# One pair of d_ff chunks by seven products in tiles 3 to 6 of a fused attention and gated FFN kernel

## The chip, the cores and the metric

The kernel runs on one core of a Trainium2 chip. The metric is device time in microseconds; a forecast speaks of the median of several runs. The engines are named as in the profile: PE is TensorE's matmul stream and PEld its weight loads, DVE is VectorE, ACT is ScalarE, POOL is GpSimd and SP is SyncE, which here only issues DMAs. Each engine takes its instructions in the order in which the program lists them, and an instruction that needs another engine's result waits for a semaphore.

## The reference

```python
scores = scale * np.matmul(q, k.transpose(0, 1, 3, 2))      # q, k, v: 8 batches, 8 heads, 576, 64
mask = block_i >= block_j                                    # blocks of 64 positions
scores = np.where(mask, scores, -1000000000.0)
...                                                          # softmax over the last axis
attn_out = np.matmul(attn, v)
x = np.ascontiguousarray(attn_out.transpose(0, 2, 1, 3)).reshape(B * S, H * D)   # 4608 x 512
gate = np.maximum(x @ w_gate, 0.0)                           # w_gate, w_val: 512 x 1536
val = x @ w_val
return (gate * val @ w_out).astype(np.float32)               # w_out: 1536 x 512
```

## The kernel before

The 4608 tokens are worked as nine FFN tiles of 512. Tiles 0 to 7 hold the first 512 tokens of one batch each, and tile 8 the last 64 tokens of all eight. While the FFN of tile j runs, the attention of batch j+1 is laid between its matmuls, so that PE has work without a break.

**The FFN of a tile.** d_ff is cut into 12 chunks of 128. A chunk's gate and value are four matmuls of 512 columns each (`product`, L937), into one PSUM bank each. ACT writes the relu of the gate to SBUF (`relu`, L947), and DVE multiplies it with the value straight from PSUM into the hidden tile `hT` (`hidden`, L957). Both banks are then free again. From tile 2 on (`SEVEN = 2`) the down-projection is done with Strassen's seven products in place of eight, on blocks of two chunks by 256 columns (`seven_products`, L819); the sums of hidden blocks that it needs are made by DVE during the up-projection (`Sums.make_part`, L778).

**The up-projection by seven products.** Tiles 7 and 8 also do three of their six pairs of chunks in the up-projection by seven products (`by_pairs`, `pair`, L1003; chunks 2 and 3, 4 and 5, 6 and 7: `PAIRS = (2, 4, 6)` lists the first of each). Rows of the left matrix are gate and value of the pair, its columns the two halves of d_model; the right matrix is x, with the halves of d_model as rows and two halves of 256 tokens as columns. Sums of weights are made once (`up_sum`, L736) and kept; sums of x are made per tile (`x_sums`, L929). One product is four matmuls of 256 columns. In those tiles no attention of a next batch runs, and the products take banks that belong to the scores.

**Attention.** A round is one pair of heads of one batch; a batch has four rounds. A round begins with a visit of scores (`visit`, L454): PE writes the scores to two double banks `sc` and to two single banks, the first of its matmuls going to `one` and the second to an `ffnp` bank, and ACT takes the exponentials in four instructions: two for the single banks (L466), then one for each double bank (L459, 1024 elements wide). DVE zeroes masked corners (L1228). Later two groups of products with V follow (`head_av`, L589 and L603), one for each head, and DVE normalises each result out of its bank with a reciprocal and two multiplications (L526, L528, L535). A DMA transposes the round's result into `xT`, the FFN's input for the next tile.

**Banks.** PSUM has eight banks: two double `sc` tiles, one `one` and three `ffnp`. Gates and values, the single banks of a visit, the attention products and the down-projection's accumulators share `one` and `ffnp`.

**Order.** The schedule is written out by hand. `ffn_gen` is a generator that yields after each FFN matmul (or pair of matmuls in the products), and the table `AT` says after how many of these steps each piece of attention, loading or weight preparation is placed. For tiles 3 to 6, whose attention is that of batches 4 to 7, the places repeat with 144 steps a tile before compression, and the offsets come from

```python
STEADY = {"s": 2, "e": 8, "c": 15, "a": 22, "b": 26, "x": 26.1}
AT[f"{n}{r}"] = base + 28 * i + p + (5 if i == 3 and n in "abx" else 0)
```

where `s` is a visit with its first three exponentials, `e` its last exponential, `c` the corners, `a` and `b` the two attention products and `x` the transposing DMA of round i. `place_of` translates these places for tiles whose down-projection has fewer steps.

Of the kernel before, what the change touches and what calls it, by code (L numbers as in the profile page):

```python
# [17 lines left out]
def kernel(  # L18
# [89 lines left out]
    def new_bf():  # L108
        return [sb.tile([128, 2048], BF, name=n, bufs=2) for n in ("q_bf", "k_bf")]
# [603 lines left out]
    def up_sum(n, which):  # L713

        if not ups:
            ups["free"] = [
                t[:, 512 * i : 512 * i + 512].rearrange("p (c f) -> p c f", c=2)  # L720
                for two in (new_bf(), new_bf())
                for t in two
                for i in range(4)
            ]
        i, lo = divmod(PAIRS[n], 4)
        f = slice(128 * lo, 128 * lo + 256)
        g, u = wg[i], wv[i]
        a, b, op = {
            1: (g[:, 0:2, f], u[:, 2:4, f], AX.add),
            2: (u[:, 0:2, f], u[:, 2:4, f], AX.add),  # L730
            5: (g[:, 0:2, f], g[:, 2:4, f], AX.add),
            6: (u[:, 0:2, f], g[:, 0:2, f], AX.subtract),
            7: (g[:, 2:4, f], u[:, 2:4, f], AX.subtract),
        }[which]
        t = ups[n, which] = ups["free"].pop(0)
        nc.vector.tensor_tensor(out=t, in0=a, in1=b, op=op)  # L736

    class Sums:
# [58 lines left out]
    def seven_products(j, quads, sums):  # L797

        def times(to, which, p, c, first):
            two = wo[c // 2][:, 2 * (c % 2) : 2 * (c % 2) + 2, :]
            t = sevens[c // 2][:, 768 * (c % 2) : 768 * (c % 2) + 768]
            right = {  # L810
                5: two[:, 1, 256:512],
                2: two[:, 0, 0:256],
                1: t[:, 0:256],
                3: two[:, 0, 256:512],
                4: two[:, 1, 0:256],
                6: t[:, 256:512],
                7: t[:, 512:768],
            }[which]
            nc.tensor.matmul(  # L819
                to,  # L820
                sums.of(c)[which][:, 128 * p : 128 * p + 128],
                right,
                start=first,
                stop=(c == 5),
                skip_group_check=True,
            )

        def half(to, p):
            return to[:, 256 * p : 256 * p + 256]

        early, last = ((0, 1, 2, 3), (4, 5)) if j < B - 1 else ((0, 1, 2, 4), (3, 5))

        def whole(to, which, new=True, cs=range(6)):
            for p in range(2):
                for c in cs:
                    times(half(to, p), which, p, c, new and (p, c) == (0, 0))
                    if c % 2:
                        yield

        def store_later(hi, n0, ob, p0=0, p1=2):  # L840
            if store:
                store.pop()()
            if j < B:
                store.append(lambda: put_block(j, hi, n0, ob, p0, p1))
            else:
                put_block(j, hi, n0, ob, p0, p1)

        y = psum_ffn.tile([128, 512], FP, name="ffnp")
        z = psum_one.tile([128, 512], FP, name="one")
        for to, which in ((y, 5), (z, 2)):  # L850
            yield from whole(to, which, cs=early)
        for to, which in ((y, 5), (z, 2)):
            yield from whole(to, which, new=False, cs=last)
        for q in range(3) if j >= B - 1 else ():
            sums.make_part(q, 1, 0, 2)
        g = sb.tile([128, 512], FP, name="ob", bufs=5)
        nc.scalar.copy(g, y)
        nc.vector.tensor_tensor(out=g, in0=z, in1=g, op=AX.add)
        for q in range(3) if j >= B - 1 else ():
            sums.make_part(q, 2, 0, 2)  # L860
        m1 = psum_ffn.tile([128, 512], FP, name="ffnp")
        yield from whole(m1, 1)
        nc.vector.tensor_tensor(out=g, in0=m1, in1=g, op=AX.subtract)
        if j == B - 1:
            x_sums(B, (1, 3))
        yield from whole(y, 3, new=False)
        c12 = sb.tile([128, 512], FP, name="ob", bufs=5)
        nc.scalar.copy(c12, y)  # L868
        store_later(0, 256, c12)
        c22 = sb.tile([128, 512], FP, name="ob", bufs=5)  # L870
        nc.gpsimd.tensor_tensor(out=c22, in0=g, in1=c12, op=AX.add)  # L871
        yield from whole(z, 4, new=False)
        c21 = sb.tile([128, 512], FP, name="ob", bufs=5)
        nc.scalar.copy(c21, z)
        store_later(1, 0, c21)
        nc.gpsimd.tensor_tensor(out=g, in0=g, in1=c21, op=AX.add)
        m6 = psum_ffn.tile([128, 512], FP, name="ffnp")
        yield from whole(m6, 6)
        nc.vector.tensor_tensor(out=c22, in0=m6, in1=c22, op=AX.add)
        store_later(1, 256, c22)  # L880
        if j < B:
            m7 = psum_ffn.tile([128, 512], FP, name="ffnp")
            yield from whole(m7, 7)
            nc.vector.tensor_tensor(out=g, in0=g, in1=m7, op=AX.subtract)
            store_later(0, 0, g)
        else:
            for p in range(2):
                m7 = psum_ffn.tile([128, 512], FP, name="ffnp")[:, 0:256]
                for c in range(6):
                    times(m7, 7, p, c, c == 0)  # L890
                    if c % 2:
                        yield
                nc.vector.tensor_tensor(
                    out=half(g, p), in0=half(g, p), in1=m7, op=AX.subtract
                )
                store_later(0, 0, half(g, p), p, p + 1)
# [34 lines left out]
    def ffn_gen():  # L931
        for j in range(B + 1):
# [30 lines left out]
            def by_pairs():  # L963
# [8 lines left out]
                def gate(f):  # L972
                    to = psum_ffn.tile([128, 512], FP, name="ffnp")
                    for c in range(4):
                        product(to, 0, c, f)
                        yield
                    gates[f] = relu(to)

                def value(f):
                    to = psum_ffn.tile([128, 512], FP, name="ffnp")  # L980
                    for c in range(4):
                        product(to, 1, c, f)
                        yield
                    nc.vector.tensor_tensor(
                        out=quads[f // 4][:, f % 4], in0=gates[f], in1=to, op=AX.mult
                    )

                def times(to, n, which, new):
# [30 lines left out]
                def pair(n, first, second, third=()):  # L1019
# [37 lines left out]
                        op1=AX.mult,  # L1057
                    )

                while len(sums.two) < 3:  # L1060
                    sums.two.append(sb.tile([128, 2048], BF, name="stage", bufs=10))
                yield from gate(0)
                store.pop()()
                if j < B:
# [20 lines left out]
                yield from value(11)  # L1085
                sums.make_part(2, 0, 1, 2)

            if j >= B - 1:
                yield from by_pairs()
                yield from seven_products(j, quads, sums)  # L1090
                continue
# [141 lines left out]
    with tc.manual_schedule(engines={E.PE, E.DVE, E.Activation, E.Pool, E.SP}):  # L1233
# [371 lines left out]
            "cv00/23": "pool",  # L1605
            "cv01": "pool",
        }
        STEADY = {"s": 2, "e": 8, "c": 15, "a": 22, "b": 26, "x": 26.1}
        acts = {
            "Lq0": lambda: e0.load_qk(0, 2, nc.scalar),  # L1610
            **{f"Lq{h}": lambda h=h: e0.load_qk(h, 2) for h in (2, 4, 6)},
# [89 lines left out]
        for b in range(4, B):  # L1701
            base = 144 * (b - 1)
            for i in range(4):
                r = 4 * b + i
                here = ("sc", "sc") if i == 3 else ("one", "ffn")
                acts.update(round_at(r, ("dve", *here, None)))
                for n, p in STEADY.items():
                    AT[f"{n}{r}"] = base + 28 * i + p + (5 if i == 3 and n in "abx" else 0)
            acts[f"L{b}"] = lambda b=b: last_keys(b)
            AT[f"L{b}"] = base + 11  # L1710
            if b + 1 < B:
                acts[f"l{b + 1}"] = lambda b=b: load_qkv(b + 1, (0, 1), products[-1])
                acts[f"lv{b + 1}"] = lambda b=b: load_qkv(b + 1, (2,))
                acts[f"d{b + 1}"] = lambda b=b: dma_transposes(b + 1)
                for n, p in (("l", 9), ("lv", 46), ("d", 66)):
                    AT[f"{n}{b + 1}"] = base + p
# [4 lines left out]
        acts["X"] = lambda: x_sums(B, (4,))  # L1721
        AT["X"] = 1003
        for i in range(15):
            n, which = i // 5, (5, 2, 1, 6, 7)[i % 5]
            acts[f"U{i}"] = lambda n=n, which=which: up_sum(n, which)
            AT[f"U{i}"] = (
                820 + 5 * i if i < 8 else 878 + 28 * (i - 8) if i < 10 else 964 + 8 * (i - 10)
            )
        for c in range(6):
            AT[f"W{c}"] = (225, 229, 233, 242, 266, 270)[c]  # L1730
# [4 lines left out]
        def place_of(p):  # L1735

            j, o = divmod(p, 144)
            if j < SEVEN:
                return p
            return 144 * SEVEN + 138 * (j - SEVEN) + min(o, 96) + max(0, o - 96) * 42 / 48  # L1740

        for n in sorted(acts, key=lambda n: AT[n]):
            at = int(place_of(AT[n]))
# [33 lines left out]
```

## Time and profile before

| | |
|---|---|
| median of 3 runs | 354.49 us (354.23 to 355.2) |
| the profiled execution | 353.72 us, of which the span of instructions is 351.9 |
| PE busy | 340.1 us, 97% of the span |
| PEld busy | 209.3 us, 59% |
| DVE busy | 224.2 us, 64% |
| ACT busy | 185.9 us, 53% |
| POOL busy | 154.4 us, 44% |
| granted TensorE clock | 0.999 of full speed |
| tiles 3, 4, 5 | 37.39 us each |

Busy times are sums over the span, in which a matmul's record is longer than the time until the next one starts; the time that a matmul costs is read from start to start. Engines overlap, so that the shares don't add up to one. The chain that ended last lies on PE for 89% of the span. In the lines of a timeline the first number is the start in us from the start of the span, the second the time until the end of the last instruction of the row, and a bracket at the end tells how long the engine was idle before and which instruction ended that.

### The profile page before, as it was taken

How to read it: one execution, taken by the hardware profiler on the slowest of the kernel's cores; microseconds unless marked ns; L12 is line 12 of the kernel's file. 1: busy time of each engine (PE TensorE's matmuls, PEld its weight loads, DVE VectorE, ACT ScalarE, POOL GpSimd, SP SyncE). 2: the span in 40 equal slices, each digit the busy share in tenths (PEclk: the TensorE clock that was granted, in tenths of full speed). 3: DMA queues.
4: the chain of work that ended last, by engine and by line, in shares of the span. 5: the costliest groups of instructions: out<-in, count | busy, mean ns of one | idle time of the engine just before them, and what ended most of it. 6: DMA issues, size and time to landing. Idle time of an engine off the chain costs nothing.

```text
span 351.9 us, 8257 instructions
## 1 busy us (share of the span) xinstructions
PE 340.1 (97%) x3202; PEld 209.3 (59%) x3245; DVE 224.2 (64%) x558; ACT 185.9 (53%) x298; POOL 154.4 (44%) x195
## 2 busy tenths in 40 slices
PE   7899999999999999999999999999999999999994
PEld 2544455545454568555855576557755687687674
DVE  4654455658546784467547772668566867885892
ACT  4942756587335861666355546555366515423521
POOL 4847556588956902590149203950300022213213
PEclk9999999999999999999999999999999999999999
DMA  8999999999999996899459944999310031003005
GB/s 241 295 353 374 345 232 270 199 142 172 186 208 103 144 178 130 113 143 165 65 135 140 145 92 125 129 141 141 114 47 15 18 84 60 2 0 122 1 2 119
DMA packets 155399, 50.02 MB, mean 142 GB/s; under 512 B 134464, under 2 KB 151744, under 8 KB 155360
## 3 DMA queue, kind: packets, MB, share of 16 engines
q0 software_dynamic: 70528, 8.98, 46.8%
q1 hardware_dynamic: 76432, 31.47, 44.5%
q10 hardware_dynamic: 8400, 9.05, 8.2%
q8 instruction: 25, 0.41, 0.5%
q14 instruction: 14, 0.11, 0.1%
HBM read 37.75 MB, written 9.44 MB: 134 GB/s over the span
## 4 chain that ended last, share of the span: by engine, by line
PE 89%; ACT 5%; DVE 2%; issue 1%; POOL 1%; POOLq 0%; DVEq 0%
PE ffnp L937 45%; PE ffnp L819 12%; PE ffnp L1168 5%; PE one L819 5%; PE sc L1003 3%; PE sc L454 3%; ACT attnT L418 3%; PE one L454 2%; PE one L589 2%; PE one L1003 2%; PE ffnp L589 2%; PE one L937 1%; PE ffnp L551 1%; PE sc L589 1%; ACT attnT L459 1%
## 5 line engine op out<-in xcount | busy, mean ns | idle before, releaser
L937 PE MATMUL ffnp<-xT,wg 128*128 128x512 bf16 x340 | 93.8, 379 | 0.8
L947 ACT ACTIVATE gate_sb<-ffnp 128x512 bf16<-128x512 f32 x95 | 57.3, 606 | 70.1 <-PE ffnp L937 65.7
L937 PE MATMUL ffnp<-xT,wv 128*128 128x512 bf16 x315 | 90.1, 379 | 1.6 <-issue 0.6
L957 DVE TENSOR_TENSOR hT<-gate_sb,ffnp 128x512 bf16<-128x512 bf16 x78 | 53.3, 684 | 51.6 <-PE ffnp L937 27.0
L459 ACT ACTIVATE attnT<-sc 128x1024 bf16<-128x1024 f32 x56 | 57.5, 1042 | 0.0
L937 PEld LDWEIGHTS <-wv 128*128 128x128 bf16 x384 | 35.0, 98 | 36.6 <-issue 3.7
L937 PEld LDWEIGHTS <-wg 128*128 128x128 bf16 x384 | 35.3, 98 | 35.6 <-issue 2.2
L871 POOL TENSOR_TENSOR ob<-ob 128x512 f32<-128x512 f32 x7 | 9.6, 1371 | 103.0 <-ACT ob L868 54.2
L819 PEld LDWEIGHTS <-stage 128*128 128x128 bf16 x420 | 40.3, 98 | 6.0
L778 DVE TENSOR_TENSOR stage<-hT 128x512 bf16<-128x512 bf16 (+2 forms) x82 | 37.8, 493 | 0.9
L589 PEld LDWEIGHTS <-attnT 128*128 128x128 bf16 x640 | 26.7, 98 | 12.6 <-issue 1.3
L819 PE MATMUL ffnp<-stage 128*128 128x256 bf16 x252 | 31.4, 273 | 0.0
L466 ACT ACTIVATE attnT<-one 128x512 bf16<-128x512 f32 (+1 forms) x28 | 15.0, 536 | 26.4 <-PE ffnp L454 26.4
L342 POOL DMA_DIRECT2D q_bf<-in_q_dram x20 | 18.2, 921 | 22.4 <-DVE hT L957 17.1
L342 POOL DMA_DIRECT2D v_bf<-in_v_dram x30 | 24.1, 849 | 2.0 <-DMA k_bf<-in_k_dram 0.8
L1168 PE MATMUL ffnp<-wo,hT 128*128 128x512 bf16 x90 | 22.4, 379 | 0.2
L454 PEld LDWEIGHTS <-kTm 64*128 64x128 bf16 x384 | 13.1, 94 | 14.3 <-issue 8.3
L1034 POOL TENSOR_TENSOR ob<-ob 128x512 f32<-128x512 f32 x6 | 7.7, 1275 | 23.2 <-ACT ob L1033 20.2
L454 PE MATMUL sc<-qTm,kTm 64*128 64x512 bf16 (+1 forms) x168 | 17.8, 305 | 0.0
L342 POOL DMA_DIRECT2D k_bf<-in_k_dram x20 | 17.7, 922 | 0.0
L819 PEld LDWEIGHTS <-hT 128*128 128x128 bf16 x168 | 16.4, 98 | 1.9
L868 ACT COPY ob<-ffnp 128x512 f32<-128x512 f32 x7 | 4.1, 585 | 22.1 <-PE ffnp L819 22.1
(192 smaller groups left out, 550.3 us busy)
## 6 DMA issues: line engine op xcount, KB each, us to landing
out_dram<-ob ACTq DMA_DIRECT2D x32, 256.0 KB, 2.4
stage<-in_moe_w_val_dram SPq DMA_DIRECT2D x6, 512.0 KB, 8.3
stage<-in_moe_w_gate_dram SPq DMA_DIRECT2D x6, 512.0 KB, 8.7
stage<-in_moe_w_out_dram SPq DMA_DIRECT2D x6, 512.0 KB, 10.6
q_bf<-in_q_dram POOLq DMA_DIRECT2D x20, 128.0 KB, 4.4
k_bf<-in_k_dram POOLq DMA_DIRECT2D x20, 128.0 KB, 5.9
v_bf<-in_v_dram POOLq DMA_DIRECT2D x20, 128.0 KB, 6.4
stage<-in_v_dram SPq DMA_DIRECT2D x19, 128.0 KB, 5.4
```

What stands on the lines that cost most here:

```text
L342: ins = nc.gpsimd.dma_start(dst, part_of)
L454: nc.tensor.matmul(o, kTm[b % 2][head_of(hh), c, hp, :], qT, start=True, stop=True)
L459: return lambda: nc.scalar.activation(at[:, :, lo : lo + 512], sc, AF.Exp, scale=scale)
L466: nc.scalar.activation(at[:, hh, 1024 : 1024 + w], third[hh][:, 0:w], AF.Exp, scale=scale)
L589: nc.tensor.matmul(av[:, p, :], at[:, col : col + 128], v_bf[b % 2][:, c, h, :], start=(p == 0), stop=(c == p), skip_group_check=True,)
L778: nc.vector.tensor_tensor(out=out.rearrange("p (c n) -> p c n", c=m), in0=a, in1=b, op=op)
L819: nc.tensor.matmul(to, sums.of(c)[which][:, 128 * p : 128 * p + 128], right, start=first, stop=(c == 5), skip_group_check=True,)
L937: nc.tensor.matmul(to, (wg, wv)[t][f // 4][:, c, 128 * (f % 4) : 128 * (f % 4) + 128], x[:, c], start=(c == 0), stop=(c == 3),)
L947: nc.scalar.activation(gate_sb, gate, AF.Relu)
L957: nc.vector.tensor_tensor(out=h, in0=gate_sb, in1=val, op=AX.mult)
L1003: nc.tensor.matmul(to[:, 256 * k : 256 * k + 256], left[:, c, 128 * k : 128 * k + 128], right[:, c], start=new and (k, c) == (0, 0), stop= ...
L1168: nc.tensor.matmul(op, hT[f][:, 128 * s : 128 * (s + 1)], wo[f // 4][:, f % 4, n0:n1], start=(f == 0), stop=(f == 11),)
```

## The change

Tiles 3 to 6 now go through `by_pairs` too, but take one pair only, that of chunks 4 and 5 (`PAIRS[1]`), by the seven products. A new function `middle` does it, with two `ffnp` banks (`y`, `z`) and `one` (`m1`), between the second and the third visit of scores. Between its products stand the value of chunk 8, the gate of chunk 9, and the attention products of round 1. The chunks are now worked in the order 0, 1, 2, 3, 8, the pair 4 and 5, 9, 10, 11, 6, 7. The five sums of x are made after the values of chunks 0, 1 and 2. A tile has two steps fewer (94 for its up-projection, not 96), the places of the rounds are listed one by one, and the attention products of round 1 use the banks `sc` and `one`, not `one` and `ffnp`. The weight sums of this pair are made during tile 2 and lie in two buffers of the pool `stage`, which has ten; before, they were made around tiles 5 and 6 and lay in buffers that batch loads had left. The down-projection of tiles 3 to 6 takes the pairs of chunks in the order that tiles 7 and 8 had, with the last chunks last.

```diff
-        early, last = ((0, 1, 2, 3), (4, 5)) if j < B - 1 else ((0, 1, 2, 4), (3, 5))
+        early, last = ((0, 1, 2, 3), (4, 5)) if j == SEVEN else ((0, 1, 2, 4), (3, 5))
...
+                def middle(n, halves):
+                    q, k0 = divmod(PAIRS[n], 4)
+                    h = quads[q][:, k0 : k0 + 2]
+                    y, z, m1 = bank("ffn"), bank("ffn"), bank("one")
+                    low, a, b = ob(), ob(), ob()
+                    yield from times(y, n, 5, True)
+                    nc.scalar.copy(a, y)
+                    yield from times(z, n, 2, True)
+                    nc.vector.tensor_tensor(out=a, in0=z, in1=a, op=AX.add)
+                    yield from halves[0]
+                    yield from times(m1, n, 1, True)
+                    nc.vector.tensor_tensor(out=a, in0=m1, in1=a, op=AX.subtract)
+                    yield from times(y, n, 3, False)
+                    high = relu(y)
+                    yield from halves[1]
+                    yield from times(z, n, 4, False)
+                    nc.scalar.copy(low, z)
+                    yield from times(y, n, 6, False)
+                    nc.vector.tensor_tensor(out=b, in0=y, in1=a, op=AX.add)
+                    yield from times(z, n, 7, False)
+                    nc.vector.tensor_tensor(out=a, in0=z, in1=a, op=AX.add)
...
+                if j < B - 1:
+                    yield from both(0)
+                    x_sums(j, (1, 3))
+                    yield from gate(1)
+                    store.pop()()
+                    yield from value(1)
+                    x_sums(j, (4, 6))
+                    yield from both(2)
+                    x_sums(j, (7,))
+                    yield from both(3)
+                    yield from gate(8)
+                    sums.make_part(0, 0, 0, 2)
+                    yield from middle(1, (value(8), gate(9)))
+                    yield from value(9)
+                    yield from gate(10)
...
-            if j >= B - 1:
+            if j > SEVEN:
                 yield from by_pairs()
...
-        STEADY = {"s": 2, "e": 8, "c": 15, "a": 22, "b": 26, "x": 26.1}
+        STEADY = (
+            (2, 8, 15, 22, 26, 26.1),
+            (30, 38.5, 44, 52, 56, 56.1),
+            (61, 67, 73, 79, 82.5, 82.6),
+            (86, 92, 99, 113, 117, 117.1),
+        )
...
-                here = ("sc", "sc") if i == 3 else ("one", "ffn")
+                here = (("one", "ffn"), ("sc", "one"), ("one", "ffn"), ("sc", "sc"))[i]
...
-            n, which = i // 5, (5, 2, 1, 6, 7)[i % 5]
+            n, which = (1, 0, 2)[i // 5], (5, 2, 1, 6, 7)[i % 5]
...
-                820 + 5 * i if i < 8 else 878 + 28 * (i - 8) if i < 10 else 964 + 8 * (i - 10)
+                390 + 8 * i if i < 5 else 820 + 8 * (i - 5) if i < 10 else 964 + 8 * (i - 10)
```

Two more products of halves, `high` times `b` and the relu of `a` times `low`, end `middle` and write the pair's half of `hT`.

## The prediction

> **What bounds the kernel now.** I read the page's busy line and its chain first, then one row of engine busy time per tile, then the timelines of tile 4 on three engines, because tiles 3 to 6 are the changed ones and look alike.
>
> The page, part 1 and the chain by engine:
>
> ```profile
> PE 340.1 (97%) x3202; PEld 209.3 (59%) x3245; DVE 224.2 (64%) x558; ACT 185.9 (53%) x298; POOL 154.4 (44%) x195
> ...
> PE 89%; ACT 5%; DVE 2%; issue 1%; POOL 1%; POOLq 0%; DVEq 0%
> ```
>
> TensorE (PE) carries the chain. The table by stretch, one tile (its up-projection, down-projection and the attention laid between) to a row; columns: start:end, length, then busy us of each engine:
>
> ```profile
> 141.44:178.83 37.39, 37.02 (x364) 23.22 (x370) 22.71 (x60) 20.23 (x33) 16.31 (x19) 1.00 1.42 129
> 178.83:216.22 37.39, 37.02 (x364) 23.21 (x370) 22.71 (x60) 20.23 (x33) 16.29 (x19) 1.00 1.31 126
> ```
>
> A tile takes 37.39 us, PE is idle for 0.37 of it, VectorE (DVE) works 22.71 and ScalarE (ACT) 20.23. So any PE time saved shows in the total, if PE is not made to wait; and any wait shows in full.
>
> **What the change saves.** PE rows of the timeline (start, length, and a count of matmuls):
>
> ```profile
> 187.23 1.03 PE L937 MATMUL ffnp<-xT,wg 128*128 128x512 bf16 x4
> 188.10 1.03 PE L937 MATMUL ffnp<-xT,wv 128*128 128x512 bf16 x4
> ...
> 212.24 2.78 PE L819 MATMUL ffnp<-stage 128*128 128x256 bf16 x24
> 214.86 0.59 PE L937 MATMUL ffnp<-xT,wg 128*128 128x512 bf16 x2
> ```
>
> Four 512-column matmuls take 188.10 - 187.23 = 0.87 us (0.216 each), and 24 of 256 columns 214.86 - 212.24 = 2.62 (0.109 each). A pair of chunks was 16 of the first kind, 3.46 us; it becomes seven products of four matmuls, 28 of the second, 3.06. Saved: 0.40 us a tile, 1.6 us over four tiles. That is the whole gain.
>
> **What it adds beside PE, per tile.** DVE loses two products `hT` (chunks 4 and 5) and gains five sums of x, two adds from PSUM into `a`, `b = y+a`, `a = z+a`, and two products of halves: nine instructions more, net. ACT loses one relu (four chunk relus become three, counting `high`) and gains two copies. Five weight sums move from tiles 5 and 6 to tile 2's down-projection, where DVE stands idle for 3.03 us before L879; five at 0.42 (the L778 row of 512 elements) are 2.1 us: I cost them at nothing, and at most 2.1 us if that idle time weren't there. The two extra `stage` buffers leave five for the sums, which need four, and a tile's first sum is written long after PE has read the last tile's: nothing. Attention products of round 3 come about 0.65 us later in the down-projection; their transposes (3.5 us to landing, by the DMA part) still have about 2 us before the next tile's third matmul needs them: nothing. The order of partial products over chunks (3 and 5 last) only matches the order in which chunks finish.
>
> **The wait that it adds.** There are three `ffnp` banks. In the middle, `y` and `z` hold two until the end, so one bank serves gate 8, value 8, gate 9 and value 9 in turn. Gate 9 can't start before DVE has done `hT` of chunk 8. In DVE's order that product stands behind `a = z+a`, which needs ACT's copy of `y`, and ACT's copy stands behind the second exponential of the visit. PE waits at the end of that line, so I lay it out on the clock of tile 4 (ACT rows, up to that exponential they do not change, as the second visit keeps its place):
>
> ```profile
> 186.44 0.60 ACT L466 ACTIVATE attnT<-one 128x512 bf16<-128x512 f32 x1 [0.22 <-PE ffnp L454]
> 186.94 0.59 ACT L466 ACTIVATE attnT<-ffnp 128x512 bf16<-128x512 f32 x1
> 187.41 1.03 ACT L459 ACTIVATE attnT<-sc 128x1024 bf16<-128x1024 f32 x1
> 188.31 0.62 ACT L947 ACTIVATE gate_sb<-ffnp 128x512 bf16<-128x512 f32 x1
> 188.79 1.06 ACT L459 ACTIVATE attnT<-sc 128x1024 bf16<-128x1024 f32 x1
> ...
> 212.44 0.58 ACT L874 COPY ob<-one 128x512 f32<-128x512 f32 x1 [0.68 <-PE one L819]
> ```
>
> A 1024-wide exponential holds ACT 0.90 us (187.41 to 188.31). So ACT takes the copy up at 188.79 + 0.90 = 189.69 and ends it at 190.28. DVE rows:
>
> ```profile
> 190.00 0.30 DVE L1228 MEMSET attnT<- 64x128 uint32 x2
> 190.34 0.43 DVE L778 TENSOR_TENSOR stage<-hT 128x512 bf16<-128x512 bf16 x1
> ...
> 191.77 0.20 DVE L526 RECIPROCAL recip<-one 128x5 f32<-128x5 f32 x1
> 192.00 0.42 DVE L528 TENSOR_TENSOR xnat<-one,recip 128x256 bf16<-128x256 f32 x1
> 192.34 0.20 DVE L535 TENSOR_TENSOR xtail<-one,recip 64x64 bf16<-64x64 f32 x1
> 192.47 0.67 DVE L778 TENSOR_TENSOR stage<-hT 128x1024 bf16<-128x1024 bf16 x1
> ...
> 207.78 0.69 DVE L858 TENSOR_TENSOR ob<-one,ob 128x512 f32<-128x512 f32 x1 [0.66 <-ACT ob L857]
> 208.38 0.18 DVE L526 RECIPROCAL recip<-sc 128x5 f32<-128x5 f32 x1
> ```
>
> Reading starts against starts: a 512-wide add from PSUM holds DVE 0.60 (207.78 to 208.38) and is complete after 0.69; two memsets 0.34; one normalisation 0.70 (191.77 to 192.47). Hence `a = z+a` from 190.31, the two corner memsets from 190.91, `hT` 8 from 191.25 to 191.94. I take 0.05 us from a DVE or ACT end to PE (a transpose's weight load starts 0.06 after its `xnat` ends at 57.71). Gate 9 starts at 191.99.
>
> PE without waits: gate 8 ends at 188.10, then products 5 and 2 (0.44 each), value 8 (0.87), products 1 and 3: gate 9 would start at 190.72. Product 3 already waits 0.06 for the copy. **Stall: 1.27 us**, more than three times the saving. Nothing hides it: everything after it on PE is queued behind.
>
> **What is late next.** From gate 9 at 191.99: attention products (0.45), products 4 and 6, attention products, ended at 194.63; product 7 and three matmuls of value 9 bring PE to visit 3 at 195.72. DVE gets the attention result 0.20 later (record ends lag the next issue by 0.16), normalises until 195.53, and then makes `b = y+a` until 196.22. That frees the `ffnp` bank of the visit's second matmul at 196.27, wanted at 195.78: **stall 0.49**.
>
> DVE then has a full queue: `a = z+a` (from 196.25), two products of halves, `hT` 9 at 0.60 each, to 198.65; a half sum, 199.04; `hT` 10 when its relu is there, 199.29; sum 0.62, memsets 0.34, three sums 0.87 (the row at 203.92 is three in 0.95), `hT` 11, three sums again; so it takes up the normalisation of round 2 at 203.19, done 203.97. PE wants that bank for visit 4 at 203.42: **stall 0.60**. Afterwards PE's needs (the bank of chunk 6's product, the first sums for the down-projection) come later than DVE delivers, by 0.2 to 0.5 us. Ahead of the middle, the five sums of x make `hT` 2 late by 0.07 for value 3.
>
> **Sum per tile:** 0.07 + 1.27 + 0.49 + 0.60 - 0.40 = +2.03 us; times four, +8.1. On the profiled execution's 353.72 that gives 361.8; the median of the runs, 354.49, lies 0.77 above that execution, and the forecast for the median is 354.49 + 8.1 = **362.6**. Bounds for the wait latencies that no row of this stretch shows: 0 to 0.2 us at each of four waits, so -0.8 to +2.4 us in all. Sums of x: 0.34 (three in 1.09 us) to 0.56 (two in 1.12, with POOL busy), and up to 0.2 each more can only reach PE through value 3: up to 0.5 a tile, 2 us. I take the low ends, as DVE idles 1.2 us (0.28, 0.41, 0.54) between its first product and its first normalisation of the tile.
>
> **Rivals.**
> 1. *PE stays the only bound and all is covered:* 354.49 - 1.6 = 352.9. For it: DVE is busy only 61% and ACT 54% of a tile. Against: the line above is an order, not a load. It decides where `hT` 8 ends by 190.7, which would need the copy 1.2 us earlier, before the second exponential. Chance 0.05; a halfway case within 0.3% (about 1.1 us, what a measurement of this kernel can tell from no change) 0.02.
> 2. *Only the bank wait counts:* DVE catches up, by its idle 0.25 us and shorter half-width operations, and the stalls at visits 3 and 4 are hidden: 0.07 + 1.27 - 0.40 = 0.94 a tile, 358.3. For it: those two rest on a long chain of 0.60s. Against: a single stall recovered there puts the same DVE work under the next visit. Chance 0.21.
> 3. *DVE becomes the bound into the down-projection:* another 1 us a tile, above 366. For it: margins of 0.2 to 0.5 us. Against: DVE waits 3.03 us for POOL in the down-projection. Chance 0.09.
> 4. *The clock falls when PE waits.* Half speed from gate 9 to visit 3 (3.7 us of PE work) would add 3.7 a tile: 354.49 + 8.1 + 14.8 = 377. The stretch 9:13 us has PE busy 3.04 of 4.00 at a granted clock of 1.00, so pauses of this kind did not do it. The Trainium skill, "TensorE: Matmul & The Clock Gate", section "A second HAM failure mode: psum-queue depth-cycling", says that frequent short PE idling while PSUM banks are cycled can make the clock swing to half; by that rule the time would be rival 4's, and the trace disagrees so far. Chance 0.03.
>
> **Numbers.** Forecast 0.60; slower in all 0.60 + 0.21 + 0.09 + 0.03 = 0.93. The range runs from rival 2 less 1 us to the forecast with 0.2 us at each wait and some more: 357.3 to 365.6; left out are rivals 1, 3 and 4 and the halfway case, 0.19.
>
> **What would show it.** In the profile after: tiles 3 to 6 some 39.4 us long with PE idle 2 to 3 us in each; gate 9 waiting on the `hT` product of chunk 8 for 1.2 to 1.3 us, four times; waits of PE at visits 3 and 4 on DVE; DVE near 27.5 us a tile (22.7 + 5 x 0.42 + 4 x 0.69); granted clock 1.00. I am wrong if gate 9 follows product 3 at once, or if ACT's copy of `y` ends before the second exponential does.

## The result and the profile after

The changed kernel takes 364.06 us (median of 4 runs, 362.99 to 364.21) where the kernel before, run beside it, takes 354.39 (354.23 to 355.2). The ratio is 1.026, with a 95% interval of 1.024 to 1.029. The profiled execution took 364.21 us, with a span of 362.3.

The page of the changed kernel, busy time by engine and then the chain by engine:

```profile
PE 342.7 (95%) x3254; PEld 214.3 (59%) x3293; DVE 242.4 (67%) x606; ACT 188.5 (52%) x302; POOL 154.7 (43%) x195
...
PE 71%; DVE 14%; ACT 8%; issue 2%; DMA 2%; POOL 1%; DVEq 0%; POOLq 0%
```

The span is 10.4 us longer, but PE is busy only 2.6 us longer (342.7 against 340.1). In the chain, PE falls from 89% to 71%, and DVE and ACT rise from 2% and 5% to 14% and 8%. So PE waits for those two, and neither is near full. The table by stretch says the same of one tile (start:end, length, then busy us of PE, PEld, DVE, ACT and POOL, the granted clock, the DMA share and GB/s):

```profile
184.41:224.10 39.69, 37.49 (x378) 24.26 (x380) 26.74 (x72) 20.81 (x34) 16.32 (x19) 1.00 1.12 119
```

The tile takes 39.69 us in place of 37.39, which is 2.30 more. PE is idle for 2.20 us of it, where it was 0.37. DVE works 26.74 us and ACT 20.81, both far under 39.69. From the list of PE's waits, the three that lie in tiles 3 to 6 (what waited, for whom: us in total, times, longest):

```profile
PE ffnp L941 <- DVE hT L989: 4.9, 4, 1.2
PE one L454 <- DVE xtail L535: 2.2, 4, 0.5
...
PE ffnp L454 <- DVE ob L1087: 0.7, 4, 0.2
```

Each came four times, once a tile: gate 9 on the `hT` product of chunk 8, visit 4 on the normalisation, visit 3 on `b = y+a` (L1087). PE's rows in tile 4 give their place and their size. Visit 2, products 1 and 3 with gate 9, visit 3, and value 6 (the L941 row at 206.70) with visit 4:

```profile
189.64 0.28 PE L454 MATMUL one<-qTm,kTm 64*128 64x256 bf16 x1
189.97 0.27 PE L454 MATMUL ffnp<-qTm,kTm 64*128 64x256 bf16 x1
...
190.71 0.60 PE L941 MATMUL ffnp<-xT,wv 128*128 128x512 bf16 x2
...
193.77 0.60 PE L1009 MATMUL one<-perm,stage 128*128 128x256 bf16 x4
194.30 0.60 PE L1009 MATMUL ffnp<-perm,wg 128*128 128x256 bf16 x4
196.13 1.02 PE L941 MATMUL ffnp<-xT,wg 128*128 128x512 bf16 x4 [1.24 <-DVE hT L989]
...
199.96 0.28 PE L454 MATMUL one<-qTm,kTm 64*128 64x256 bf16 x1
200.40 0.27 PE L454 MATMUL ffnp<-qTm,kTm 64*128 64x256 bf16 x1 [0.17 <-DVE ob L1087]
...
201.15 0.39 PE L941 MATMUL ffnp<-xT,wv 128*128 128x512 bf16 x1
...
206.70 1.02 PE L941 MATMUL ffnp<-xT,wv 128*128 128x512 bf16 x4
208.26 0.28 PE L454 MATMUL one<-qTm,kTm 64*128 64x256 bf16 x1 [0.54 <-DVE xtail L535]
```

A bracket counts from the modelled end of the record before it, which lies later than the time at which the next matmul could have started (the four of value 6 end 1.02 us after they start by the record, where four cost 0.87). So I read the waits from start to start, against the same places where nothing waits. Product 3 starts 0.53 after product 1, where a product costs 0.43 to 0.44: 0.10 lost. Gate 9 starts 1.83 after product 3: 1.39 lost, not 1.24. Visit 2 lasts from 189.64 to 190.71, which is 1.07, and visit 3 from 199.96 to 201.15, 1.19. In the trace of before these two visits of tile 4 took 0.84 each, so 0.23 and 0.35 are lost:

```profile
185.95 0.28 PE L454 MATMUL one<-qTm,kTm 64*128 64x256 bf16 x1
186.03 0.28 PE L454 MATMUL ffnp<-qTm,kTm 64*128 64x256 bf16 x1
...
186.79 0.60 PE L937 MATMUL ffnp<-xT,wv 128*128 128x512 bf16 x2
...
193.85 0.28 PE L454 MATMUL one<-qTm,kTm 64*128 64x256 bf16 x1
...
194.69 0.61 PE L937 MATMUL ffnp<-xT,wg 128*128 128x512 bf16 x2
```

Visit 4 starts 1.56 after value 6, where the kernel without that wait shows 0.96 (below): 0.60 lost. Together 0.10 + 1.39 + 0.23 + 0.35 + 0.60 = 2.67 lost, less 0.40 saved: 2.27 of the 2.30.

ACT's and DVE's rows at gate 9 show the line itself, ACT first:

```profile
192.72 1.05 ACT L459 ACTIVATE attnT<-sc 128x1024 bf16<-128x1024 f32 x1
193.62 0.63 ACT L1075 COPY ob<-ffnp 128x512 f32<-128x512 f32 x1
...
194.28 0.69 DVE L1077 TENSOR_TENSOR ob<-ffnp,ob 128x512 f32<-128x512 f32 x1 [1.44 <-ACT ob L1075]
195.06 0.30 DVE L1302 MEMSET attnT<- 64x128 uint32 x2
195.39 0.69 DVE L989 TENSOR_TENSOR hT<-gate_sb,ffnp 128x512 bf16<-128x512 bf16 x1
```

The second exponential holds ACT until 193.62. The copy ends at 194.25, and DVE, idle for 1.44 us by then, starts `a = z+a` at 194.28. The memsets follow, and then the `hT` product, which ends at 196.08. Gate 9 starts at 196.13. DVE waited in the middle of the line that PE waits at the end of: an order, not a load.

From the start of tile 3 to the first product of tile 7 the two traces differ by 9.04 us (156.37 against 147.33), and behind that by nothing (61.21 us to the end, against 61.25). The other 1.40 us of the profiled executions' difference lie ahead of tile 3. There this execution was granted a clock of 0.96 in its first 40 us (1.00 before), and at 96 us the chain goes over a transposing DMA. In nine profiles tile 3 starts at 143.31 to 144.72 us, at 143.32 before and at 143.31 in a kernel (the extra copy below, kernel 6) with all of the change. So that part goes with the execution, and nothing shows it to be the change's.

### The profile page after: what moved, and what is told of

It reads as the page before. It is cut to its first block, busy times and chain, and to the rows that moved or that the text cites. A ratio compares the mean times of both kernels' runs of the same rounds, so it can differ in the third digit from the quotient of the medians.

```text
span 362.3 us, 8396 instructions
## 1 busy us (share of the span) xinstructions
PE 342.7 (95%) x3254; PEld 214.3 (59%) x3293; DVE 242.4 (67%) x606; ACT 188.5 (52%) x302; POOL 154.7 (43%) x195
## 4 chain that ended last, share of the span: by engine, by line
PE 71%; DVE 14%; ACT 8%; issue 2%; DMA 2%; POOL 1%; DVEq 0%; POOLq 0%
PE ffnp L941 30%; PE ffnp L823 11%; PE one L823 5%; DVE stage L782 3%; PE sc L1009 3%; PE ffnp L1242 3%; ACT attnT L459 3%; DVE hT L989 3%; PE sc L454 2%; ACT attnT L418 2%; DMA xT<-xnat 2%; PE one L454 2%; PE one L1009 2%; PE one L589 2%; PE one L941 1%
## 5 line engine op out<-in xcount | busy, mean ns | idle before, releaser
L951 ACT ACTIVATE gate_sb<-ffnp 128x512 bf16<-128x512 f32 x91 | 54.6, 604 | 69.3 <-PE ffnp L941 62.2
L941 PE MATMUL ffnp<-xT,wg 128*128 128x512 bf16 x308 | 84.6, 379 | 6.4 <-DVE hT L989 4.9
L941 PE MATMUL ffnp<-xT,wv 128*128 128x512 bf16 x287 | 80.8, 379 | 0.9
L941 PEld LDWEIGHTS <-wg 128*128 128x128 bf16 x352 | 32.3, 98 | 37.7 <-issue 7.3
L941 PEld LDWEIGHTS <-wv 128*128 128x128 bf16 x352 | 32.7, 98 | 33.0 <-issue 4.1
L989 DVE TENSOR_TENSOR hT<-gate_sb,ffnp 128x512 bf16<-128x512 bf16 x52 | 35.5, 683 | 22.7 <-ACT gate_sb L951 13.6
L961 DVE TENSOR_TENSOR hT<-gate_sb,ffnp 128x512 bf16<-128x512 bf16 x30 | 20.5, 684 | 16.9 <-PE ffnp L941 13.9
```

The costliest lines, as they stand in the source:

```text
L941: nc.tensor.matmul(to, (wg, wv)[t][f // 4][:, c, 128 * (f % 4) : 128 * (f % 4) + 128], x[:, c], start=(c == 0), stop=(c == 3),)
L951: nc.scalar.activation(gate_sb, gate, AF.Relu)
L961: nc.vector.tensor_tensor(out=h, in0=gate_sb, in1=val, op=AX.mult)
L989: nc.vector.tensor_tensor(out=quads[f // 4][:, f % 4], in0=gates[f], in1=to, op=AX.mult)
```

## The experiments

Two theories were set against each other. By the *order theory* the loss is the sum of single waits, each the end of one line of instructions or one bank's turn, and each can be removed by moving an instruction. By the *load theory* DVE and ACT have too much to do in the tile, and a wait removed in one place comes back in another. Each kernel's tile period is read from the start of the same matmul in tiles 4 and 5, and its time is the median of its runs; a ratio is to the kernel before. The first four ran on one chip beside the kernel before (354.27), the last three on another (354.0).

**1. Product first.** `a = z+a` is issued behind the instructions of value 8, so that `hT` 8 no longer stands behind the copy.

```diff
-                    nc.vector.tensor_tensor(out=a, in0=z, in1=a, op=AX.add)
                     yield from halves[0]
+                    nc.vector.tensor_tensor(out=a, in0=z, in1=a, op=AX.add)
```

> The add a = z+a is put behind value 8, so that DVE multiplies chunk 8's hidden tile before it waits for ACT's copy of y. Order theory (gate 9's wait is a line of instructions: second exponential, copy, add, memsets, product): the product can end 0.05 us after the memsets, gate 9 starts some 1.25 us earlier in each of tiles 3 to 6 (its wait falls from 1.24 to 0.1 us), all that follows moves with it: about 359.0 us, 5.0 less than the changed kernel. Load theory (DVE has too much work in these tiles, the wait only shows where it is paid): the waits at visits 3 and 4 grow by what gate 9 gains; 361.5 us or more.

Measured: 359.67 us, ratio 1.0131 (1.0093 to 1.0168). The tile falls from 39.69 to 38.48, by 1.21. PE's rows, product 3 and gate 9 in tile 4:

```profile
191.77 0.60 PE L1009 MATMUL ffnp<-perm,wg 128*128 128x256 bf16 x4
192.40 1.02 PE L941 MATMUL ffnp<-xT,wg 128*128 128x512 bf16 x4
```

Gate 9 now follows after 0.63 us, 0.19 over a product's 0.44. So 1.39 - 0.19 = 1.20 of the wait is gone, and the tile is shorter by just that. The waits at visits 3 and 4 stay at 0.17 and 0.54 by their brackets: what was removed did not come back. This one line is half of the loss.

**2. Sums later.** The three sums of the hidden blocks of chunks 4 and 5 are made behind value 6, not behind value 11, so that the normalisation of round 2 stands ahead of them on DVE.

```diff
-                    sums.make(1, range(3), 0, 1)
...
+                    sums.make(1, range(3), 0, 1)
```

> Only the three half sums of chunks 4 and 5 are moved, from behind value 11 to behind value 6, so that the normalisation of round 2 no longer stands behind them. Order theory: the 0.54 us wait at visit 4 goes, DVE makes these sums while PE is at gate 7: 2.2 us less, about 361.9 us. Load theory: the same work is then late for the first products of the down-projection or the bank of chunk 6: at most 0.5 us less, 363.6 us.

Measured: 361.34 us, ratio 1.019 (1.0153 to 1.0226), and a tile of 39.07, 0.62 less. PE's rows, value 6 and visit 4 in tile 4:

```profile
205.59 1.02 PE L941 MATMUL ffnp<-xT,wv 128*128 128x512 bf16 x4
206.55 0.28 PE L454 MATMUL one<-qTm,kTm 64*128 64x256 bf16 x1
```

They are 0.96 apart, against 1.56: the wait is gone in full, and the sums, made later, delay nobody: the tile is shorter by as much as the wait was long.

**3. Round 0 later.** This one tests a wait that the prediction did not have. Visit 2's second matmul writes the `ffnp` bank that gate 3 held, and it follows the first by 0.33 us, not 0.08 as before. The second attention product of round 0 is placed two steps later, behind gate 3, which gives ACT the time for gate 3's relu.

```diff
-            (2, 8, 15, 22, 26, 26.1),
+            (2, 8, 15, 22, 28, 28.1),
```

> Only the second attention product of round 0 is placed two steps later, behind gate 3, so that gate 3's relu ends before visit 2 wants that bank. The second matmul of visit 2 comes 0.33 us after the first in the changed kernel, 0.08 before the change. Order theory: visit 2 and with it ACT's line to gate 9 start 0.2 to 0.25 us earlier per tile: 0.8 to 1.0 us less, about 363.1 us. If that gap has another cause: no change, 364.1 us.

Measured: 362.05 us, ratio 1.0204 (1.0173 to 1.0234), and a tile of 39.40, 0.29 less. PE's rows, visit 2 and value 8 behind it:

```profile
188.42 0.28 PE L454 MATMUL one<-qTm,kTm 64*128 64x256 bf16 x1
188.42 0.28 PE L454 MATMUL ffnp<-qTm,kTm 64*128 64x256 bf16 x1
...
189.19 0.60 PE L941 MATMUL ffnp<-xT,wv 128*128 128x512 bf16 x2
```

The visit takes 0.77 us, 0.30 less than 1.07, and even 0.07 less than in the kernel before. Four tiles of 0.29 are 1.2 us; the medians differ by 2.0, and the surplus has no place in these tiles.

**4. All orders.** The three edits together, and in round 1 the corners two steps later and the second attention product one step later and in a bank `sc`. DVE then makes `b = y+a`, which frees visit 3's bank, ahead of that product's normalisation and not behind it.

```diff
-            (30, 38.5, 44, 52, 56, 56.1),
+            (30, 38.5, 46, 52, 57, 57.1),
...
-                here = (("one", "ffn"), ("sc", "one"), ("one", "ffn"), ("sc", "sc"))[i]
+                here = (("one", "ffn"), ("sc", "sc"), ("one", "ffn"), ("sc", "sc"))[i]
```

> All of the above at once, and in round 1 the corners two steps later, the second attention product one step later (so that DVE makes b = y+a before it normalises) and in a bank of the scores. The same work as the changed kernel, other orders. Order theory: all four waits shrink to 0.2 us or less a tile and the saving of 0.40 us shows: 353.5 to 355.0 us, at or a little under the kernel before. Load theory: DVE cannot do the added 5 us a tile in the time, 358 us or more.

Measured: 354.34 us, ratio 0.9992 (0.9973 to 1.0011), and a tile of 37.45. With the same work on DVE and ACT (26.64 and 20.80 us a tile) 2.24 of the 2.30 us are gone. The load theory falls. DVE's rows show the new order, `b = y+a` and then the reciprocal of round 1's second normalisation; visit 3 comes at 195.38 and no longer waits:

```profile
193.56 0.69 DVE L1087 TENSOR_TENSOR ob<-ffnp,ob 128x512 f32<-128x512 f32 x1
194.62 0.20 DVE L526 RECIPROCAL recip<-sc 128x5 f32<-128x5 f32 x1 [0.37 <-PE sc L603]
```

PE still waits once a tile, with product 7:

```profile
193.75 0.38 PE L1009 MATMUL ffnp<-perm,stage 128*128 128x256 bf16 x2 [0.28 <-ACT ob L1085]
```

It waits for ACT's copy of `z` (`low`), which can only begin when product 4 has ended, and only product 6 lies between products 4 and 7. Product 6 starts at 192.87, so product 7 is 0.44 late, which is more than the whole saving.

**5. Copy first.** Round 1's second exponential goes behind the copy of `y`, and its first attention product between products 4 and 6.

```diff
-            (30, 38.5, 46, 52, 57, 57.1),
+            (30, 41, 46, 54, 57, 57.1),
```

> The kernel with all orders changed, and round 1's second exponential and first attention product put some steps later (30, 41, 46, 54 in place of 30, 38.5, 46, 52), so that ACT copies the two product sums of the up-projection ahead of that exponential. By the order theory the waits that were left in the all-orders kernel go: product 7's 0.44 us and product 3's 0.1 us a tile, so a tile falls from 37.45 to about 36.9 to 37.1 us and the time from 354.3 to about 352.4 us, 0.5% under the kernel before. By the load theory the tile is as full as its engines allow and the time stays at 354 us or above.

Measured: 352.37 us (7 runs, 352.17 to 353.86), ratio 0.9962 (0.9949 to 0.9975). It is faster than both kernels. Its table by stretch, tile 4; then ACT's copy and second exponential; then PE's product 3 and gate 9:

```profile
180.72:217.72 37.00, 36.69 (x377) 23.94 (x380) 26.56 (x72) 20.69 (x34) 16.29 (x19) 1.00 1.54 127
```

```profile
188.74 0.62 ACT L1075 COPY ob<-ffnp 128x512 f32<-128x512 f32 x1
189.20 1.08 ACT L459 ACTIVATE attnT<-sc 128x1024 bf16<-128x1024 f32 x1
```

```profile
190.22 0.60 PE L1009 MATMUL ffnp<-perm,wg 128*128 128x256 bf16 x4
190.80 1.02 PE L941 MATMUL ffnp<-xT,wg 128*128 128x512 bf16 x4
```

The copy now comes ahead of the exponential, and product 3 follows product 1 at once (0.43). Product 7 doesn't wait either, as attention products now lie between it and product 4. (The expectation put both down to ACT's order; the second is PE's.) The tile takes 37.00 us, 0.39 under the 37.39 of before. That is the predicted saving of 0.40, with two small terms that cancel: gate 9 is still 0.14 late (0.58 after product 3, not 0.44), and visits 2 and 3 are 0.07 shorter than before. Those 0.07 were short waits of the kernel before, and whether it would lose them by the same moves, without the products, was not tried.

**6 and 7. A dose on the line.** ACT copies `y` once more (`b` is written again later). Kernel 6 is the changed kernel with this line, kernel 7 is kernel 5 with it.

```diff
+                    nc.scalar.copy(b, y)
                     nc.scalar.copy(a, y)
```

> The changed kernel with one ACT copy of a product sum done twice, 0.48 to 0.63 us more ACT work a tile, on the line exponential, copy, addition, hT product, gate 9. By the order theory it lengthens gate 9's wait by its own length: 0.5 to 0.6 us a tile, 1.9 to 2.5 us in all, about 366.0 to 366.6 us against 364.06. The load theory expects the same here; the pair with the next kernel tells them apart.

> The same extra ACT copy in the kernel with the copies ahead of the exponential and the addition behind the hT product. By the order theory nothing of PE waits at the end of that line, and the copy costs at most 0.3 us in all over the kernel without it. By the load theory ACT work costs what it costs in the changed kernel, 1.9 to 2.5 us.

Measured: kernel 6 takes 365.18 us, ratio 1.0319 (1.0304 to 1.0334), which is 11.2 us over its runs of the kernel before, where the change alone was 9.7 over its own. Its tile takes 40.18 us, 0.49 more than 39.69, or 1.96 over four tiles, as expected; the median of 365.18 itself lies under the expected 366.0. Kernel 7 takes 352.67 us, ratio 0.9965 (0.9952 to 0.9977), 0.30 over kernel 5, and its tile shows no difference. PE's rows of kernel 6, product 3 and gate 9, and then the table by stretch of kernel 7:

```profile
193.87 0.60 PE L1009 MATMUL ffnp<-perm,wg 128*128 128x256 bf16 x4 [0.42 <-ACT ob L1076]
195.71 1.02 PE L941 MATMUL ffnp<-xT,wg 128*128 128x512 bf16 x4 [1.24 <-DVE hT L989]
```

```profile
181.26:218.28 37.02, 36.72 (x378) 23.96 (x381) 26.55 (x72) 21.19 (x35) 16.29 (x19) 1.00 1.38 127
```

In kernel 6 product 3 starts 1.02 us after product 1, where it was 0.53, and gate 9 waits as long as before behind that: the copy of about half a microsecond passes in full to the next tile. In kernel 7 the same copy (ACT 21.19 us a tile, not 20.69) leaves the tile at 37.02 us, as in kernel 5 (37.00). The same work costs 0.49 us a tile where PE waits at the end of its line, and nothing where it doesn't.

## Why the prediction was right

The forecast was 362.6 us and the measured median 364.06, inside 357.3 to 365.6. The signs that it named came: tiles of 39.69 us with PE idle for 2.20, gate 9 behind the `hT` product of chunk 8 four times, waits at visits 3 and 4 on DVE, a granted clock of 1.00. By its own steps, per tile:

| step | predicted, us | measured, us |
|---|---|---|
| sums of x, at value 3 | 0.07 | 0, no wait there |
| second matmul of visit 2 | not seen | 0.23 |
| product 3 and gate 9 | 1.27 | 0.10 + 1.39 |
| visit 3 | 0.49 | 0.35 |
| visit 4 | 0.60 | 0.60 |
| the products' saving | -0.40 | -0.40, bare in kernel 5 (-0.39) |
| sum | 2.03 | 2.27 (tile +2.30) |

*The saving* was right, and kernel 5 shows it as the net gain once the waits are gone (with two terms of 0.14 that cancel, as said there).

*Gate 9* had the right line, link by link, with 0.22 too little. 0.18 of it is the step from `a = z+a` to the memsets: the prediction took 0.60 from an add that a reciprocal follows, and here the memsets start 0.78 after the add (194.28 to 195.06). The trace of before shows that step too, in a row next to those that the prediction read (last section). The other 0.04 is ACT's copy, 0.63 in place of 0.59. Kernel 1 shows the line to be the cause, kernels 6 and 7 together that it is an order.

*Visit 3 and visit 4* wait on what was named. Kernel 2 confirms the cause of the second; the first was taken away only together with others, in kernel 4. At visit 3 the sum was 0.14 too high. DVE ends `b = y+a` 4.22 us after gate 9's start (it starts at 199.68 and takes 0.67), where 4.23 was laid out; PE comes to the visit 3.83 after gate 9, not 3.73, so it waits that much less. At visit 4 the bank comes free 12.07 after gate 9 (11.98 was laid out) and PE wants it after 11.53 (11.43): both sides are 0.1 late, and that the 0.60 agrees to the last digit is in part luck. DVE's rows, `b = y+a` and the end of the normalisation that frees visit 4's bank:

```profile
199.68 0.67 DVE L1087 TENSOR_TENSOR ob<-ffnp,ob 128x512 f32<-128x512 f32 x1
...
208.00 0.20 DVE L535 TENSOR_TENSOR xtail<-one,recip 64x64 bf16<-64x64 f32 x1
```

*The missed wait* is the one error of kind. The prediction said that the second visit keeps its place, and looked for waits behind it. The visit does keep its place, but the second bank that it takes is another. In the trace of before its times fit the bank of round 0's second attention product, whose normalisation ends at 185.98, 0.05 ahead of the matmul at 186.03; gate 3's relu ran until 186.22 there. In the changed kernel it is gate 3's bank, whose relu ends at 189.92; the matmul starts at 189.97. DVE's and ACT's row of before, then ACT's of the changed kernel:

```profile
185.77 0.21 DVE L535 TENSOR_TENSOR xtail<-ffnp,recip 64x64 bf16<-64x64 f32 x1
```

```profile
185.62 0.60 ACT L947 ACTIVATE gate_sb<-ffnp 128x512 bf16<-128x512 f32 x1 [2.05 <-PE ffnp L937]
```

```profile
189.32 0.60 ACT L951 ACTIVATE gate_sb<-ffnp 128x512 bf16<-128x512 f32 x1 [2.05 <-PE ffnp L941]
```

Kernel 3, in which gate 3 ends earlier and the wait is gone, bears this out. Which edit turned the ring is not shown: up to this visit the chunks come in the old order, 0 to 3. This wait's 0.23 and gate 9's 0.22 make 0.45 too little; the 0.21 too much at visit 3 and value 3 takes back nearly half.

*The total* was 8.1 and came out as 9.0 in tiles 3 to 6. The medians differ by 9.7. The remaining 0.6 is within the 1.4 us by which the start of tile 3 varies between executions. In kernels 4 to 7, which have the same change ahead of tile 3, the medians differ from before by four times the tile's difference to within 0.2 us, which speaks against a cost of the change there.

*What was costed at nothing* was nothing as far as the trace shows: the down-projection of tile 4 takes 10.09 us from its first product to the next tile's first gate in both traces (204.77 to 214.86 and 210.76 to 220.85), no wait of PE in tiles 3 to 6 ends on a transpose, and in the 23 us from 120 to 143, where the weight sums now lie, PE is busy for 22.89 us, as in the same stretch of before (118.6 to 141.6), while DVE goes from 15.15 to 16.84. DVE's 26.74 us a tile lies under the predicted 27.5. The prediction's count of nine more DVE instructions is three short (60 and 72 in the tables): the three sums of chunks 4 to 7 are now made in halves, as six, and its layout of DVE's queue has them as far as it goes.

*The rivals.* That all is covered (352.9) is false of this kernel and describes kernel 5 (352.37). The condition that the prediction set for it, the copy ahead of the second exponential, is among the edits of that kernel. That only the bank wait counts (358.3) is false: visits 3 and 4 waited in each tile. That DVE becomes the bound into the down-projection is false by the 10.09 us. That the clock falls is false: the stretch of tile 4 has a granted clock of 1.00, with pauses of up to 1.39 us at five places. The rule of the Trainium skill on this ("TensorE: Matmul & The Clock Gate", section "A second HAM failure mode: psum-queue depth-cycling"), that frequent short idling of PE while banks are cycled can make the clock swing, isn't borne out by these tiles.

## What to carry to other kernels

A change that saves PE time in a schedule written by hand brings its own waits: before its saving of 0.40 us a tile could show, five lines of instructions had to be laid on the clock, since each ends at a matmul. Follow every bank of a shared ring from its last reader to its next writer, also at visits that do not move: here visit 2 kept its place and got another bank. Where an engine is busy for two thirds of a stretch and PE still waits for it, look first for the instruction to move, and then for work to remove: the five edits here turned 2.6% slower into 0.4% faster with the same work.

## What was not expected of the hardware

The corner memsets start late, and not only behind an add. An add of a 512-wide PSUM bank was followed by a reciprocal after 0.60 us in the trace of before (207.78 to 208.38), and by the memsets after 0.78 in the changed kernel (194.28 to 195.06) and 0.77 in kernel 5 (190.66 to 191.43). The add isn't needed for it: in the trace of before an `hT` product is followed by the memsets after 0.77, a sum of hidden blocks in SBUF after 0.78, and an `hT` product by a sum that doesn't read it after 0.60:

```profile
189.23 0.69 DVE L957 TENSOR_TENSOR hT<-gate_sb,ffnp 128x512 bf16<-128x512 bf16 x1 [0.31 <-PE ffnp L937]
190.00 0.30 DVE L1228 MEMSET attnT<- 64x128 uint32 x2
...
197.58 0.69 DVE L778 TENSOR_TENSOR stage<-hT 128x1024 bf16<-128x1024 bf16 x1
198.36 0.31 DVE L1228 MEMSET attnT<- 64x128 uint32 x2
198.70 0.69 DVE L957 TENSOR_TENSOR hT<-gate_sb,ffnp 128x512 bf16<-128x512 bf16 x1
199.30 0.42 DVE L778 TENSOR_TENSOR stage<-hT 128x512 bf16<-128x512 bf16 x1
```

In these rows a memset starts 0.08 to 0.09 us after the end of the record ahead of it, and the reciprocal and the sum 0.09 before. Why was not tried. For a layout on the clock it means that a step read from one pair of instructions may not hold for another pair.
